# Value matmuls on half the array's columns each, in a two-layer attention and MLP kernel

## The chip, the cores and the metric

The kernel runs on one core of a Trainium2 chip. The metric is the device time of one execution in microseconds; where several runs are shown, their median. A core has a matrix engine (PE, with its weight loads shown apart as PEld), a vector engine (DVE), a scalar engine (ACT), a general engine (POOL) and a queue engine for transfers (SP). Each works through its own list of instructions in order, and they wait for one another through semaphores. Matmuls write to PSUM, which has 8 banks of 128 partitions by 512 floats.

## What is computed

Four residual blocks in a row on one sequence of 2048 rows of 512: attention, MLP, attention, MLP, with the same weights for both attentions and for both MLPs.

```python
def _A_ref(x, wqkv, wo):
    B, S, D = x.shape
    H = 32; Dh = D // H
    qkv = (x @ wqkv).reshape(B, S, 3, H, Dh).transpose(2, 0, 3, 1, 4)
    q, k, v = qkv[0], qkv[1], qkv[2]
    scores = jnp.einsum("bhqd,bhkd->bhqk", q, k) * Dh ** -0.5
    p = _softmax(scores, axis=-1)
    o = jnp.einsum("bhqk,bhkd->bhqd", p, v)
    return o.transpose(0, 2, 1, 3).reshape(B, S, D) @ wo

def _B_ref(x, w1, w2):
    return jnp.einsum("bsf,fd->bsd", _silu(jnp.einsum("bsd,df->bsf", x, w1)), w2)

x = x + _A_ref(_layernorm(x), wqkv, wo)
x = x + _B_ref(_layernorm(x), w1, w2)
x = x + _A_ref(_layernorm(x), wqkv, wo)
x = x + _B_ref(_layernorm(x), w1, w2)
```

S is 2048, D 512, the MLP's width 1792; there are 32 heads of 16. All inputs are bf16.

## The kernel before

Everything stays on the chip: the activations `x_sb`, the weights, and per layer the keys `KT` and the values `vs`. Each of the two layers runs one loop over units (line 725). A unit is a block of 512 queries (c, four of them), a group of four heads (hb, eight of them) and a block of 128 keys (kt, sixteen of them), so there are 512 units per layer and 1024 in all.

A unit has three parts. The scores (`emit_s`, line 612) are four matmuls, one per head, each over 17 rows of the array that start at row 0, 32, 64 or 96; their outputs, 128 keys by 512 queries, go in pairs into two PSUM tiles `s_ps` of two banks each, from a pool of three. The exponentials (line 732) are two ACT instructions, one per pair of heads (`pr` 0 and 1), each over 128 by 1024, from `s_ps` to the bf16 tile `p_sb`, of which there are four. The value matmuls (`emit_pv`, line 624) multiply `p_sb` by the values and add up over all sixteen key blocks in one PSUM bank `o_ps`, of which there is one. Each head owns 32 of the 128 partitions of `o_ps`: 16 for its output, one for the sum of its probabilities. To get four heads into one bank, the values are laid out in `vd`: for each head j a block of 128 columns that is zero but for the 16 columns of that head and a column of ones at 32j + 16. So every value matmul uses all 128 columns, and three quarters of them multiply zeros. `vd` holds four key blocks, in two slots; POOL refills a slot with four copies (`vd_fill`, line 142) every four units, once its last reader is done.

The order of the work on PE, ACT and DVE is the order in which the program emits it (`manual_schedule`, line 633). In the loop a unit emits its two exponentials, then the scores of the next unit, then value matmuls, then at most one piece of background work. The value matmuls of a unit's second pair are held over: at kt 1 to 15 the block has the held pair of the unit before and the first pair of this one, four matmuls in all. At kt 0 only the held pair of the last head group is emitted, after which DVE copies `o_ps` out (`finish_heads`, line 722) and the bank is reused; at kt 1 the block has six matmuls, both pairs of kt 0 and the first of kt 1. `p_sb` and `s_ps` turn over in this order: a score tile is free when the exponential that read it has ended, a probability tile when its value matmuls have.

Background work comes from two lists. `must` holds the projections that the next head group needs (`k_piece` line 255, `q_piece` lines 359 and 383, `v_piece` line 316, `heads_piece` line 397), `side` what follows for the query block before: the output projection (`epilogue_pieces`, lines 423 and 432), normalization, the MLP (`ffn_pieces`: up projection line 450, tanh on ACT line 484, down projection line 457) and the next layer's values. A rate spreads these steps over the remaining units (`pump_one`). After the loop the last query block's MLP runs by itself (`last_chunk`).

Of the kernel before, what the change touches and what calls it, by code (L numbers as in the profile page):

```python
# [12 lines left out]
BF16 = mybir.dt.bfloat16  # L13
# [5 lines left out]
def kernel(  # L19
# [10 lines left out]
    nc = tc.nc  # L30
# [5 lines left out]
    P = 128  # L36
    H = 32
    DH = D // H
    assert D == 512 and DH == 16 and S % 512 == 0 and F % P == 0
    CT = D // P  # L40
    TT = S // P
# [6 lines left out]
    NG = 4  # L48
    NR = 2
# [3 lines left out]
    xpool = ctx.enter_context(tc.tile_pool(name="xpool", bufs=1))  # L53
# [61 lines left out]
    for pad, i in ((wk_pad, 1), (wq_pad, 0)):  # L115
        for ct in range(CT):
            nc.gpsimd.tensor_copy(
                out=pad[:, ct, :, 0:DH],
# [10 lines left out]
    vs = [vpool.tile([P, TT, D], BF16, name=f"v{i}", tag="v") for i in range(2)]  # L129
    vdq = []  # L130
    for i in range(NR):
        vd = xpool.tile([P, NG, 4, P], BF16, name=f"vd{i}")
        nc.gpsimd.memset(vd[:], 0.0)
        for j in range(4):
            nc.gpsimd.memset(vd[:, :, j, 32 * j + DH : 32 * j + DH + 1], 1.0)
        vdq.append(vd)


    def vd_fill(va, hb, g, slot):
        for j in range(4):  # L140
            h = 4 * hb + j
            nc.gpsimd.tensor_copy(  # L142
                out=vdq[slot][:, :, j, 32 * j : 32 * j + DH],
                in_=va[:, NG * g : NG * (g + 1), DH * h : DH * (h + 1)],
            )

# [159 lines left out]
    def amax_bm(hb):  # L306
        nc.vector.tensor_reduce(
            out=amax[:, hb : hb + 1], in_=KT[:, hb, :], axis=AX.X, op=ALU.max,
            apply_absolute_value=True,
        )  # L310
        nc.vector.tensor_scalar_mul(out=Bm[:, hb, :], in0=E[:, :], scalar1=amax[:, hb : hb + 1])
# [192 lines left out]
    def next_pieces(c, xnTs, va):  # L504
        cell = {}
        pieces = ln_steps(c, cell)
        for tq in range(4):
            pieces.append(v_piece(lambda: cell["xnT"], 4 * c + tq, va))

        def keep():  # L510
            xnTs[c] = cell["xnT"]

        pieces.append([keep])
        return pieces
# [91 lines left out]
    def add(q, pieces):  # L606
        q += [list(p) for p in pieces]

    def emit_s(QT, hb, kt):
        tiles = [wide("s_ps") for _ in range(2)]  # L610
        for j in range(4):
            nc.tensor.matmul(  # L612
                tiles[j // 2][:, j % 2, :],
                lhsT=KT[32 * j : 32 * j + VS, hb, kt * P : (kt + 1) * P],
                rhs=QT[32 * j : 32 * j + VS, :],
                start=True,
                stop=True,
            )
        return tiles

    def emit_pv(o_ps, p_sb, kt, pr):
        for jj in range(2):
            j = 2 * pr + jj
            nc.tensor.matmul(  # L624
                o_ps[:, :],
                lhsT=vdq[kt // NG % NR][:, kt % NG, j, :],
                rhs=p_sb[:, jj, :],
                start=(kt == 0 and j == 0),
                stop=(kt == TT - 1 and j == 3),
            )  # L630

    ordered = {mybir.EngineType.PE, mybir.EngineType.Activation, mybir.EngineType.DVE}
# [44 lines left out]
    def v_first_out(c, on_act):  # L677
        dst = vs[0][:, 4 * c : 4 * c + 4, 0 : D // 2]
        if on_act:
            nc.scalar.copy(dst, v_pss[c][:, :, :])  # L680
        else:
            nc.vector.tensor_copy(out=dst, in_=v_pss[c][:, :, :])
# [21 lines left out]
    for L in range(2):  # L704
        va = vs[L]
        last = L == 1
        nxt = [None] * NQC
        QTn = [[None] * HB for _ in range(NQC)]
        units = [(c, hb, kt) for c in range(NQC) for hb in range(HB) for kt in range(TT)]
        attn = None  # L710
        o_ps = None
        pend = []
        acc = 0.0
        s_now = emit_s(QTs[0][0], 0, 0)
        if L == 0:
            v_first_out(NQC - 1, False)
        for i in range(NR):
            vd_fill(va, 0, i, i)

        def finish_heads(o_ps, hb, attn):  # L720
            oT = opool.tile([P, 512], BF16, name="oT", tag="oT")
            nc.vector.tensor_copy(out=oT[:], in_=o_ps[:])  # L722
            return heads_piece(oT, hb, attn)

        for u, (c, hb, kt) in enumerate(units):
            if kt == 0 and hb == 0:
                new_attn = apool.tile([P, 4, D], BF16, name="attn", tag="attn")

            ps = []
            for pr in range(2):  # L730
                p_sb = ppool.tile([P, 2, 512], BF16, name="p_sb", tag="p")
                nc.scalar.activation(  # L732
                    p_sb[:].rearrange("p a b -> p (a b)"),
                    s_now[pr][:].rearrange("p a b -> p (a b)"),
                    ACT.Exp,
                    scale=float(SCALE),
                )
                ps.append(p_sb)

            if u + 1 < len(units):  # L740
                nc_, nhb, nkt = units[u + 1]
                s_now = emit_s(QTs[nc_][nhb], nhb, nkt)

            if kt == 0:
                for args in pend:
                    emit_pv(*args)
                heads = None
                if o_ps is not None:
                    heads = finish_heads(o_ps, (hb - 1) % HB, attn)
                if hb == 0:  # L750
                    if c > 0:
                        add(side, epilogue_pieces(c - 1, attn))
                        add(side, ffn_pieces(c - 1, emit_out=last))
                        if not last:
                            add(side, next_pieces(c - 1, nxt, vs[1]))
                    attn = new_attn
                o_ps = oppool.tile([P, 512], FP32, name="o_ps", tag="o")
                pend = [(o_ps, ps[0], 0, 0), (o_ps, ps[1], 0, 1)]
                if c == 0 and hb + 1 < HB:
                    add(must, [k_piece(xnTs, k, hb + 1) for k in range(NQC)])  # L760
                    add(must, [[lambda hb=hb: amax_bm(hb + 1)]])
                if hb + 1 < HB:
                    add(must, [q_piece(xnTs, c, hb + 1, QTs)])
                elif c + 1 < NQC:
                    add(must, [q_piece(xnTs, c + 1, 0, QTs)])
                if L == 0 and c == 0 and hb < HB // 2:
                    for tt in range(4 * hb, 4 * hb + 4):
                        add(must, [v_piece(lambda tt=tt: xnTs[tt // 4], tt, va, D // 2, D)])
                if c == NQC - 1 and hb == 1 and not last:
                    add(side, [k_first_piece(nxt, k) for k in range(NQC - 1)])  # L770
            else:
                pend.append((o_ps, ps[0], kt, 0))
                for args in pend:
                    emit_pv(*args)
                pend = [(o_ps, ps[1], kt, 1)]

            if kt % NG == 0 and u > 0 and u + NG * (NR - 1) < len(units):
                _, fhb, fkt = units[u + NG * (NR - 1)]
                vd_fill(va, fhb, fkt // NG, fkt // NG % NR)

            if kt == 1:
                if heads is not None:
                    must.insert(0, list(heads))
                continue
            left = TT - kt - (2 if kt == 0 else 0)
            remaining = left + (TT - 2) * (HB - 1 - hb)
            rate = (steps(must) + steps(side) + len(cur) + 2 * (HB - 1 - hb)) / remaining
            rate = max(rate, (steps(must) + len(cur)) / max(left - 1, 1))
            acc = min(acc + rate, 1.99)
            if acc >= 1.0:  # L790
                pump_one()
                acc -= 1.0
            if kt == TT - 2:
                while must:
                    pump_one()
        for args in pend:
            emit_pv(*args)
        run([finish_heads(o_ps, HB - 1, attn)])
        assert not must
        while side or cur:  # L800
            pump_one()
        mvs = last_chunk(NQC - 1, attn, emit_out=last)
        if not last:
            c = NQC - 1
            nxt[c] = xtpool.tile([P, CT, 512], BF16, name="xnT", tag="xt")
            for half in range(2):
                apply_transpose(mvs[half], 4 * c, [2 * half, 2 * half + 1], nxt[c], half == 0)
            xnTs, QTs = nxt, QTn
            q_first = q_piece(xnTs, 0, 0, QTs, first=True)
            k_ps = k_first_mm(xnTs[c])  # L810
            q_first[0]()
            k_first_out(k_ps, c)
            amax_first()
            for tt in (4 * c, 4 * c + 2):
                v_two(xnTs[c], tt, vs[1])
            q_first[1]()
# [28 lines left out]
```

## Time and profile before

| | |
|---|---|
| median of 3 runs | 2133.42 us (2133.16 to 2134.91) |
| the profiled execution | 2134.4 us |
| its span, first to last instruction | 2132.6 us |
| mean granted clock of PE | 0.983 |
| first exponential of layer 1, of layer 2 | 60.6 us, 1103.9 us |
| PE busy, ACT busy | 92%, 93% |

In the profile a group of instructions is one line: source line, engine, operation, output and inputs by the program's names, shapes, count; then the busy time and the mean of one in ns; then how long the engine stood idle just before such instructions, and what ended most of it. Busy times are the union of records. Matmuls are pipelined and a record shows about 379 ns of one, while the next can start 216 ns after it, so PE's busy share isn't its load. The slices divide the span in 40 equal parts and give tenths. PEclk is the share of full speed that the clock throttle granted to PE. Some value matmuls have no record (3919 of 4096).

These are the groups of the background work, which the change doesn't touch:

```profile
L457 PE MATMUL y_ps<-w_sb,hT 128*128 128x512 bf16 x440 | 115.8, 379 | 0.4
L450 PE MATMUL h_ps<-xnT,w_sb 128*128 128x512 bf16 x333 | 85.9, 379 | 0.2
L255 PE MATMUL k_ps<-xnT,wk_pad 128*128 128x512 bf16 x251 | 69.5, 398 | 3.2 <-DVE xnT L664 1.6
L359 PE MATMUL q_ps<-xnT,wq_pad 128*128 128x512 bf16 x253 | 66.4, 383 | 0.2
L484 ACT ACTIVATE t_sb<-h_ps 128x512 f32<-128x512 f32 x84 | 59.2, 705 | 0.0
```

### The profile page before, as it was taken

To read this page: it belongs to the slowest core of one execution; us is meant where nothing else is said; L and a number is where in the kernel's file an instruction comes from. 1 tells how busy PE (TensorE), PEld (TensorE's weight loads), DVE (VectorE), ACT (ScalarE), POOL (GpSimd) and SP (SyncE) were. 2 spreads that over 40 slices of the span, in tenths; PEclk is the share of its full clock that TensorE was granted. 3 is DMA by queue.
4 is the path that set the end of the run, shared out by engine and by line. 5 is a ranking of instruction groups with operands and counts; after the bars stand their busy time and mean duration, and the time that the engine had idled before them with its cause. 6 is when DMAs were issued, how large, how long until landed. Compare 5 with 4: busy or idle time off the path is not lost.

```text
span 2132.6 us, 28924 instructions
## 1 busy us (share of the span) xinstructions
PE 1964.2 (92%) x10533; PEld 722.5 (34%) x10737; DVE 549.2 (26%) x1132; ACT 1990.4 (93%) x2207; POOL 244.9 (11%) x1054
## 2 busy tenths in 40 slices
PE   4999999999999999999789999999999999999996
PEld 2333333333333333333343333333333333333334
DVE  4333223112322133212342322221113111131104
ACT  3899999999999999999649999999999999999992
POOL 2011111111111111111001111111111111111110
PEclk8999999999999999999889999999999999999998
DMA  4000000000000000000000000000000000000000
GB/s 148 1 1 1 1 1 1 1 1 1 1 1 1 1 1 1 1 1 1 1 1 1 1 1 1 1 1 1 4 8 1 1 1 8 3 1 1 3 6 13
DMA packets 9023, 11.82 MB, mean 6 GB/s; under 512 B 432, under 2 KB 8368, under 8 KB 8880
## 3 DMA queue, kind: packets, MB, share of 16 engines
q1 hardware_dynamic: 7296, 8.39, 1.2%
q8 instruction: 84, 1.38, 0.3%
q10 hardware_dynamic: 1584, 1.57, 0.2%
q14 instruction: 59, 0.48, 0.1%
HBM read 7.86 MB, written 2.10 MB: 5 GB/s over the span
## 4 chain that ended last, share of the span: by engine, by line
PE 52%; ACT 25%; issue 20%; DVE 2%; DMA 0%; ACTq 0%; SPq 0%; POOL 0%; another core or an unknown queue 0%; POOLq 0%
PE o_ps L624 25%; ACT p_sb L732 24%; PE s_ps L612 13%; PE y_ps L457 4%; PE q_ps L359 2%; PE k_ps L255 2%; PE h_ps L450 2%; PE h_ps L563 1%; ACT xn L198 1%; PE at_ps L397 1%; PE y_ps L432 1%; DVE st L150 1%; PE v_ps L316 1%; PE q_ps L383 0%; DMA x_sb<-in_A_x_dram 0%
## 5 line engine op out<-in xcount | busy, mean ns | idle before, releaser
L732 ACT ACTIVATE p_sb<-s_ps 128x1024 bf16<-128x1024 f32 x2048 | 1915.1, 1096 | 26.1 <-PE s_ps L612 13.7
L624 PE MATMUL o_ps<-p_sb,vd 128*128 128x512 bf16 x3919 | 1038.3, 383 | 18.7 <-issue 15.1
L612 PE MATMUL s_ps<-QT,KT 17*128 17x512 bf16 x4096 | 620.5, 383 | 83.7 <-ACT p_sb L732 72.9
L624 PEld LDWEIGHTS <-vd 128*128 128x128 bf16 x4096 | 317.8, 98 | 478.4 <-issue 237.2
L142 POOL COPY vd<-v 128x64 bf16<-128x64 bf16 x1024 | 231.9, 238 | 1823.1 <-PE o_ps L624 1777.7
L612 PEld LDWEIGHTS <-KT 17*128 17x128 bf16 x4096 | 164.1, 91 | 628.5 <-issue 605.9
L485 DVE SCALAR_TENSOR_TENSOR hT<-t_sb,h_ps 128x512 bf16<-128x512 f32 x84 | 57.7, 686 | 329.0 <-ACT t_sb L484 329.0
L457 PE MATMUL y_ps<-w_sb,hT 128*128 128x512 bf16 x440 | 115.8, 379 | 0.4
L722 DVE CAST oT<-o_ps 128x512 bf16<-128x512 f32 x64 | 44.3, 691 | 175.6 <-PE o_ps L624 175.6
L450 PE MATMUL h_ps<-xnT,w_sb 128*128 128x512 bf16 x333 | 85.9, 379 | 0.2
L463 DVE SCALAR_TENSOR_TENSOR x_sb<-y_ps,x_sb 128x512 bf16<-128x512 f32 x32 | 22.1, 690 | 234.2 <-PE y_ps L457 234.2
L388 DVE CAST QT<-q_ps 128x512 bf16<-128x512 f32 x64 | 44.3, 692 | 143.6 <-PE q_ps L383 143.6
L269 DVE TENSOR_SCALAR KT<-k_ps,onescol 128x512 bf16<-128x512 f32 x56 | 42.0, 751 | 137.2 <-PE k_ps L255 136.8
L255 PE MATMUL k_ps<-xnT,wk_pad 128*128 128x512 bf16 x251 | 69.5, 398 | 3.2 <-DVE xnT L664 1.6
L374 DVE CAST qc<-q_ps 128x512 bf16<-128x512 f32 x64 | 44.3, 692 | 91.3 <-PE q_ps L359 91.3
L359 PE MATMUL q_ps<-xnT,wq_pad 128*128 128x512 bf16 x253 | 66.4, 383 | 0.2
L457 PEld LDWEIGHTS <-hT 128*128 128x128 bf16 x448 | 43.8, 98 | 52.4
L403 DVE RECIPROCAL rec<-at_ps 128x16 f32<-128x16 bf16 x64 | 16.5, 258 | 166.0 <-PE at_ps L397 166.0
L484 ACT ACTIVATE t_sb<-h_ps 128x512 f32<-128x512 f32 x84 | 59.2, 705 | 0.0
L207 PE MATMUL t_ps<-ident,xn 128*128 128x128 bf16 x72 | 10.1, 293 | 47.5 <-ACT xn L198 47.0
L450 PEld LDWEIGHTS <-w_sb 128*128 128x128 bf16 x336 | 32.9, 98 | 39.6
L150 DVE BATCH_NORM_STATS2 st<-x_sb 128x6 f32<-128x512 bf16 x64 | 43.1, 673 | 3.1 <-DMA x_sb<-in_A_x_dram 2.6
(88 smaller groups left out, 658.4 us busy)
## 6 DMA issues: line engine op xcount, KB each, us to landing
w_sb<-in_B_w_dram SPq DMA_DIRECT2D x2, 1792.0 KB, 14.7
out_dram<-x_sb SPq DMA_DIRECT2D x16, 128.0 KB, 1.7
x_sb<-in_A_x_dram SPq DMA_DIRECT2D x3, 512.0 KB, 9.5
wraw<-in_A_wqkv_dram ACTq DMA_DIRECT2D x2, 512.0 KB, 5.8
x_sb<-in_A_x_dram SPq DMA_DIRECT2D x2, 256.0 KB, 4.1
wv_sb<-in_A_wqkv_dram ACTq DMA_DIRECT2D x1, 512.0 KB, 9.5
wo_sb<-in_A_wo_dram SPq DMA_DIRECT2D x1, 512.0 KB, 9.5
```

The source lines that it names most:

```text
L142: nc.gpsimd.tensor_copy(out=vdq[slot][:, :, j, 32 * j : 32 * j + DH], in_=va[:, NG * g : NG * (g + 1), DH * h : DH * (h + 1)],)
L150: nc.vector.bn_stats(st[:], x_sb[:, tt, :])
L255: nc.tensor.matmul(ps, lhsT=wk_pad[:, ct, 4 * hb : 4 * hb + 4, :].rearrange("p h s -> p (h s)"), rhs=xnT[:, ct, :], start=(ct == 0), stop= ...
L359: nc.tensor.matmul(cell["ps"][:, :], lhsT=wq_pad[:, ct, 4 * hb : 4 * hb + 4, :].rearrange("p h s -> p (h s)"), rhs=xnTs[c][:, ct, :], star ...
L374: nc.vector.tensor_copy(out=qc[:], in_=cell["ps"][:, :])
L450: nc.tensor.matmul(ps, lhsT=w1_sb[:, ct, ft * P : (ft + 1) * P], rhs=xfT[:, ct, :], start=(ct == 0), stop=(ct == CT - 1),)
L457: nc.tensor.matmul(ps, lhsT=hT[:, ft, tq * P : (tq + 1) * P], rhs=w2_sb[:, ft, :], start=(ft == 0), stop=(ft == FT - 1),)
L484: nc.scalar.activation(t_sb[:], hc["ps"][:, :], ACT.Tanh, scale=0.5)
L485: nc.vector.scalar_tensor_tensor(out=cell["hT"][:, ft, :], in0=t_sb[:], scalar=1.0, in1=hc["ps"][:, :], op0=ALU.add, op1=ALU.mult,)
L612: nc.tensor.matmul(tiles[j // 2][:, j % 2, :], lhsT=KT[32 * j : 32 * j + VS, hb, kt * P : (kt + 1) * P], rhs=QT[32 * j : 32 * j + VS, :], ...
L624: nc.tensor.matmul(o_ps[:, :], lhsT=vdq[kt // NG % NR][:, kt % NG, j, :], rhs=p_sb[:, jj, :], start=(kt == 0 and j == 0), stop=(kt == TT - ...
L732: nc.scalar.activation(p_sb[:].rearrange("p a b -> p (a b)"), s_now[pr][:].rearrange("p a b -> p (a b)"), ACT.Exp, scale=float(SCALE),)
```

## The change

The blocks of `vd` get 64 columns per head instead of 128. Heads 0 and 1 (the first pair) write partitions 0 to 63 of `o_ps`, heads 2 and 3 partitions 64 to 127; within its half, a head still owns 32 partitions, so the layout of `o_ps` stays as it was. `emit_pv` now takes the whole list of pending pairs. It sorts their matmuls by half and emits them in turns, a matmul of the second pair first, then one of the first pair, until both lists are empty. The first matmul of each half opens its accumulation and the last one closes it. The number of matmuls, weight loads and POOL copies stays; the block at kt 0 has matmuls of one half only, the block at kt 1 two of one half and four of the other.

```diff
-        vd = xpool.tile([P, NG, 4, P], BF16, name=f"vd{i}")
+        vd = xpool.tile([P, NG, 4, 64], BF16, name=f"vd{i}")
         nc.gpsimd.memset(vd[:], 0.0)
         for j in range(4):
-            nc.gpsimd.memset(vd[:, :, j, 32 * j + DH : 32 * j + DH + 1], 1.0)
+            nc.gpsimd.memset(vd[:, :, j, 32 * (j % 2) + DH : 32 * (j % 2) + DH + 1], 1.0)
...
-                out=vdq[slot][:, :, j, 32 * j : 32 * j + DH],
+                out=vdq[slot][:, :, j, 32 * (j % 2) : 32 * (j % 2) + DH],
...
-    def emit_pv(o_ps, p_sb, kt, pr):
-        for jj in range(2):
-            j = 2 * pr + jj
+    def emit_pv(pend):
+        halves = [[], []]
+        for o_ps, p_sb, kt, pr in pend:
+            for jj in range(2):
+                halves[pr].append((o_ps, p_sb, kt, pr, jj))
+        order = []
+        while halves[0] or halves[1]:
+            for h in (1, 0):
+                if halves[h]:
+                    order.append(halves[h].pop(0))
+        for o_ps, p_sb, kt, pr, jj in order:
             nc.tensor.matmul(
-                o_ps[:, :],
-                lhsT=vdq[kt // NG % NR][:, kt % NG, j, :],
+                o_ps[64 * pr : 64 * pr + 64, :],
+                lhsT=vdq[kt // NG % NR][:, kt % NG, 2 * pr + jj, :],
                 rhs=p_sb[:, jj, :],
-                start=(kt == 0 and j == 0),
-                stop=(kt == TT - 1 and j == 3),
+                start=(kt == 0 and jj == 0),
+                stop=(kt == TT - 1 and jj == 1),
             )
...
-                for args in pend:
-                    emit_pv(*args)
+                emit_pv(pend)
```

More of the change, by code (lines that the diff above doesn't have):

```diff
@@ L772 @@
                 pend.append((o_ps, ps[0], kt, 0))
-                for args in pend:
-                    emit_pv(*args)
+                emit_pv(pend)
                 pend = [(o_ps, ps[1], kt, 1)]
@@ L795 @@
                     pump_one()
-        for args in pend:
-            emit_pv(*args)
+        emit_pv(pend)
         run([finish_heads(o_ps, HB - 1, attn)])
```

## The prediction

> **What bounds the kernel now.** I read the page's busy table first, then its slices, then the group table.
>
> ```profile
> PE 1964.2 (92%) x10533; PEld 722.5 (34%) x10737; DVE 549.2 (26%) x1132; ACT 1990.4 (93%) x2207; POOL 244.9 (11%) x1054
> ...
> PE   4999999999999999999789999999999999999996
> ...
> ACT  3899999999999999999649999999999999999992
> ...
> PEclk8999999999999999999889999999999999999998
> ...
> L732 ACT ACTIVATE p_sb<-s_ps 128x1024 bf16<-128x1024 f32 x2048 | 1915.1, 1096 | 26.1 <-PE s_ps L612 13.7
> L624 PE MATMUL o_ps<-p_sb,vd 128*128 128x512 bf16 x3919 | 1038.3, 383 | 18.7 <-issue 15.1
> L612 PE MATMUL s_ps<-QT,KT 17*128 17x512 bf16 x4096 | 620.5, 383 | 83.7 <-ACT p_sb L732 72.9
> L624 PEld LDWEIGHTS <-vd 128*128 128x128 bf16 x4096 | 317.8, 98 | 478.4 <-issue 237.2
> ```
>
> Two engines look full. Outside the start, the layer change near the middle and the tail, ACT and PE are both at nine tenths. The exponentials (L732) decide: 2048 of them, with only 26.1 us of idle in front of them in all. By the ends of their records, undisturbed ones follow each other every 0.915 us and a tanh (L484, x84) adds 0.49: 2048 x 0.915 + 84 x 0.49 = 1915 us. The two attention stretches last 979 us (first exp 60.6 to last end 1040.0) and 978 us (1103.9 to 2081.7). So about 40 us in them is ACT being late, and no quicker PE can win more than that. PE looks full because it always has a little too much; the timeline tells what one unit (four heads, one block of 128 keys) costs it.
>
> ```profile
> 1001.49 0.71 PE L612 MATMUL s_ps<-QT,KT 17*128 17x512 bf16 x4
> ...
> 1002.13 1.04 PE L624 MATMUL o_ps<-p_sb,vd 128*128 128x512 bf16 x4
> ...
> 1003.10 0.39 PE L612 MATMUL s_ps<-QT,KT 17*128 17x512 bf16 x2
> 1003.64 0.39 PE L612 MATMUL s_ps<-QT,KT 17*128 17x512 bf16 x2 [0.15 <-ACT p_sb L732]
> ```
>
> A unit lasts two exponentials, 1.83 us. The second pair of score matmuls can start only when an exp has freed its PSUM tile (the wait on ACT). From there it is 0.32 us to the first value matmul, 0.216 between value matmuls, and 0.31 from the last one back to scores (1003.10 - 1002.13 = 0.97 for the block). PE needs 0.32 + 0.97 = 1.29 us of each 1.83; background work (four matmuls of 0.216 in a heavy step) fills the rest.
>
> The third view is the clock, in stretches of 3.41 us, because that is how long the granted clock stays put.
>
> ```profile
> 119.40:122.81 3.41, 3.41 (x25) 1.61 (x23) 0.85 (x2) 3.41 (x5) 0.00 (x0) 1.00 0.02 5
> 122.81:126.22 3.41, 2.53 (x13) 0.76 (x13) 0.69 (x1) 3.41 (x4) 0.91 (x4) 1.00 0.00 0
> 126.22:129.64 3.42, 3.42 (x12) 0.98 (x11) 0.00 (x0) 2.90 (x4) 0.00 (x0) 0.50 0.00 0
> 129.64:133.05 3.41, 3.41 (x25) 1.36 (x23) 1.16 (x3) 3.18 (x5) 0.45 (x2) 1.00 0.00 0
> 153.53:156.94 3.41, 2.69 (x15) 0.77 (x13) 0.98 (x2) 3.41 (x5) 0.90 (x4) 1.00 0.00 0
> ...
> 1136.56:1139.98 3.42, 2.69 (x13) 0.85 (x14) 0.69 (x1) 3.32 (x4) 0.90 (x4) 1.00 0.00 0
> 1139.98:1143.40 3.42, 3.42 (x12) 0.99 (x11) 0.00 (x0) 3.21 (x4) 0.00 (x0) 0.50 0.02 5
> 1143.40:1146.80 3.40, 3.40 (x25) 1.34 (x23) 1.37 (x3) 2.96 (x4) 0.45 (x2) 1.00 0.00 0
> ```
>
> The columns are length, then PE, weight loads, DVE, ACT and POOL busy with their instructions, then the granted clock. Nothing here stands idle for 3 us, yet after a stretch with 13 matmuls (122.81, 1136.56) the next runs at 0.50; after one with 15 (153.53) it stays at 1.00. Counting a matmul as 0.213 us of streaming, matmuls that run together once: 122.81 has four score pairs and four value matmuls (one without a record), 1.70 us or 0.50 of the stretch; 153.53 comes to 0.53. At full clock, streaming less than about half of such a stretch costs the clock of the next. In the half-clock stretch and the one after it ACT lost 0.52 + 0.23 = 0.75 us, and 0.21 + 0.44 = 0.65 us.
>
> **The change, part by part.** *Value matmuls at 64 columns, halves alternating.* Their number stays 4096, and so do their rows and the 512 moving columns. No row shows 64 columns. The bounds on a pair: both halves start together, as the four score matmuls do on four row groups (3 to 4 ns between starts), or one after the other, 0.216 apart as now. I take together, because the score row is the nearest case of parts of the array used side by side. The block shrinks from 0.97 to 0.216 + 0.31 = 0.53 us, and a unit from 1.29 to 0.85. At kt 0 only one half has work (two matmuls, serial as now); at kt 1 six matmuls take four slots. Weight loads: 98 ns each in the shadow of a 216 ns matmul; bounds 0 and 0.098 exposed per load, I take 0.
>
> The Trainium skill, "TensorE: Matmul & The Clock Gate", Part 3, says a weight load overlaps running matmuls only where the row group differs, which speaks against this change; the L624 rows, all on the same 128 rows, load while the previous matmul runs, so the trace does not bear it out. By the rule two loads per block would be exposed, some 0.2 us, and the unit would save 0.24 instead of 0.44.
>
> *A new array switch.* Full-width work behind a value block now follows another shape. The known switch costs 0.31 - 0.216 = 0.10 us; some 450 places, 45 us of PE against 0.43 x 960 = 413 saved. It lies in PE's new slack: nothing.
>
> *Fills and clearing.* The 1024 POOL copies (238 ns) keep their size and only change place; DMAs, SP, ACT and DVE keep their instructions. The two clearings of vd (1.81 us each at 10.6) halve, but POOL then waits 13.2 us for the first value copy anyway: nothing.
>
> *The wait at kt 2.* By the ends, 18.9 of the 40 us lie before the first exp of kt 2, 64 times 0.30. It overwrites the probabilities of kt 0, which the deferred value matmuls read: freed PSUM tile, 0.05 + 0.32 to the block, 0.23 to its second matmul, 0.38 until that ends, 0.1 to ACT, 1.08 against 0.915 for the exp between. The matmul meant is now fourth in line but in the second slot: no gain (serial: 0.43 x 64 = 28 us lost).
>
> *Gain.* What remains is 40 - 19 = 21 us, of which some 6 lie in the half-clock openings of the two layers. I take 15; bounds 0 and 21.
>
> *The clock, which is late next.* A unit without background work streams two score pairs and two value slots, 4 x 0.213 = 0.85 of 1.83, or 0.47 (before: 1.28, 0.70). That is under the point where the trace loses its clock. I halved the value streaming in each of the 569 stretches of 3.41 us inside attention, by the matmul records: the median falls from 0.80 to 0.59, and 17% come under 0.50, some 25% under 0.53. A slowed stretch is itself busy enough to win the clock back, so 78 to 110 stretches are slowed; I take 90. Price of one: at half clock a bare unit is about 1.5 us, under 1.83, so 0; with a heavy step the scores come 0.05 + 0.53 + 0.96 + 4 x 0.43 + 0.1 + 0.6 = 4.0 us after an exp freed the tile and are due three exps after it, at 2.75, so 1.25. The measured pair, with four serial value matmuls and little else, is 0.65 to 0.75. I take 0.45, below it, because the block is shorter now: 90 x 0.45 = 40 us; bounds 78 x 0.1 = 8 and 110 x 0.75 = 83.
>
> The skill's Part 1 of the same page has the clock fall after an idle stretch of about 3.4 us and advises against gaps over 3 us. The two rows above fall without one, so I go by the rows. By the rule no stretch here qualifies and the sum would be 2134 - 15 = 2119.
>
> *Sum.* The profiled execution took 2134.4 us (span 2132.6 and 1.8 around it), 1.0 above the median. 2134.4 - 15 + 40 = 2159; at the median, 2158.
>
> **The rivals.** *A: faster, the clock holds.* If what the clock watches is not streaming time (the number of matmuls is unchanged), or the level is below 0.45, the 40 us drop out: 2133 - 15 = 2118. For it: 57.96 to 61.37 had about 0.46 by my count and kept its clock. Against: the two rows above. It decides from fewer than 30 slowed stretches (30 x 0.45 = 14, the gain).
>
> *B: the halves don't run side by side.* Four slots stay, kt 2 loses 28 us, and the new switches (45 us of PE, a third reaching ACT) 15: 2133 + 43 = 2176. PE stays busy and the clock holds. For it: no row shows columns split. Against: the row groups overlap.
>
> *C: gain and clock loss cancel,* 33 slowed stretches: 2133.
>
> **How the numbers follow.** Forecast 0.50, A 0.29, B 0.11, C 0.10. The forecast's own range is 2133 - 15 + 8 = 2126 to 2133 + 83 - 15 = 2201. The whole range takes in A with its gain at 21 (2112) and ends at 2200. About 0.2% (4 us) is what a measurement tells from no change. Faster 0.30 (A, a little of the forecast's low end), same 0.12, slower 0.58.
>
> **What would show it.** The PEclk row of the slices falling to 7 or 8 in attention, and 3.41 us stretches alternating 1.00 and 0.50, prove the clock step; a steady 9 proves A. Value matmuls starting in pairs a few ns apart, and blocks of 0.53 us, prove the pairing; 0.216 throughout proves B. The wait before the first exp of kt 2 should stay near 0.3 us. I am wrong if PE is seen waiting on ACT at full clock throughout.

## The result, and the profile after

The changed kernel takes 2247.98 us (median of 4 runs, 2238.95 to 2251.1) against 2133.89: slower, ratio 1.0526 with a 95% interval of 1.0512 to 1.0541. The profiled execution has a span of 2249.3 us and a mean granted clock of 0.832, where it was 0.983.

From the page of the changed kernel, three rows of the slices and the groups of the attention loop (the exponentials are now at L741, the value matmuls at L633):

```profile
PE   4898899889988999889789889898899898998897
...
ACT  3899998999999999999459998989999999998993
...
PEclk8888867898878988998877886868987879877888
...
L741 ACT ACTIVATE p_sb<-s_ps 128x1024 bf16<-128x1024 f32 x2048 | 1921.6, 1101 | 114.1 <-PE s_ps L612 66.5
L612 PE MATMUL s_ps<-QT,KT 17*128 17x512 bf16 x4096 | 711.4, 437 | 217.3 <-ACT p_sb L741 207.6
L633 PE MATMUL o_ps<-p_sb,vd 128*64 128x512 bf16 x4096 | 797.1, 457 | 0.8 <-ACT p_sb L741 0.8
```

The clock row, nearly all 9 inside attention before, now shows 6 to 8 in most slices. ACT's idle time before the exponentials went from 26.1 to 114.1 us: 66.5 of it waits for scores, 44.0 for a value matmul whose probabilities the exponential overwrites. At the same time PE's waits for ACT before the scores went from 72.9 to 207.6 us. The two now wait for each other in turn. A record of a score matmul lasts 437 ns on average and one of a value matmul 457, where both were 383 before.

At a full clock the change does what it says. This is the timeline of PE in the changed kernel, over one unit without background work:

```profile
601.51 0.39 PE L612 MATMUL s_ps<-QT,KT 17*128 17x512 bf16 x2 [0.53 <-ACT p_sb L741]
601.84 0.62 PE L633 MATMUL o_ps<-p_sb,vd 128*64 128x512 bf16 x4
602.43 0.39 PE L612 MATMUL s_ps<-QT,KT 17*128 17x512 bf16 x2
```

The block of four value matmuls begins 0.33 us after the second score pair and is back at scores after 0.59 us, where it took 0.97. By the records the four start at 601.836, 601.839, 602.076 and 602.079: two pairs, 3 ns apart within a pair. PE now needs 0.92 us of a 1.83 us unit and waits 0.53 us for ACT in each.

What follows is the clock in stretches of 3.41 us. The columns are as in the prediction (length; PE, weight loads, DVE, ACT, POOL busy with their instructions; granted clock), and the last two are DMA:

```profile
601.27:604.68 3.41, 2.62 (x16) 0.75 (x16) 2.31 (x7) 3.41 (x5) 0.46 (x2) 1.00 0.00 0
604.68:608.09 3.41, 2.91 (x12) 0.77 (x12) 1.17 (x5) 3.22 (x4) 0.48 (x3) 0.50 0.00 0
608.09:611.51 3.42, 3.42 (x17) 0.84 (x14) 1.81 (x10) 2.80 (x4) 0.00 (x0) 0.50 0.02 5
611.51:614.92 3.41, 3.41 (x16) 0.88 (x14) 0.68 (x2) 3.02 (x4) 0.47 (x2) 0.50 0.00 0
614.92:618.33 3.41, 3.11 (x24) 0.98 (x24) 2.35 (x6) 2.74 (x4) 0.53 (x2) 1.00 0.00 0
```

A thin stretch (601.27, PE recorded busy for 2.62 us, much of it single score pairs) is followed by not one but three at half clock, although PE is recorded busy all through the second and third. ACT loses 0.19, 0.62, 0.39 and then, at full clock again, 0.67 us. PE's timeline inside these stretches shows what a unit with four small transposes in it costs at half clock:

```profile
609.41 0.98 PE L612 MATMUL s_ps<-QT,KT 17*128 17x512 bf16 x4
610.33 1.06 PE L633 MATMUL o_ps<-p_sb,vd 128*64 128x512 bf16 x4
611.32 0.61 PE L397 MATMUL at_ps<-ident,oT 128*128 128x128 bf16 x4
611.86 0.61 PE L612 MATMUL s_ps<-QT,KT 17*128 17x512 bf16 x4
```

From one set of scores to the next it is 2.45 us, against 1.83 that ACT needs for the unit.

### The profile page after: what moved, and what is told of

Read it like the earlier page. It is cut to its first block, busy times and chain, and to the rows that moved or that the text cites. A ratio compares the mean times of both kernels' runs of the same rounds, so it can differ in the third digit from the quotient of the medians.

```text
span 2249.3 us, 29064 instructions
## 1 busy us (share of the span) xinstructions
PE 1963.7 (87%) x10737; PEld 567.6 (25%) x10737; DVE 549.2 (24%) x1132; ACT 2005.2 (89%) x2207; POOL 249.3 (11%) x1054
## 4 chain that ended last, share of the span: by engine, by line
PE 61%; ACT 27%; issue 9%; DVE 3%; DMA 0%; ACTq 0%; SPq 0%
ACT p_sb L741 25%; PE o_ps L633 22%; PE s_ps L612 18%; PE y_ps L457 4%; PE q_ps L359 4%; PE h_ps L450 3%; PE k_ps L255 3%; PE v_ps L316 1%; PE h_ps L563 1%; PE y_ps L432 1%; PE at_ps L397 1%; ACT t_sb L484 1%; ACT xn L198 1%; PE q_ps L383 1%; DVE st L150 1%
## 5 line engine op out<-in xcount | busy, mean ns | idle before, releaser
L741 ACT ACTIVATE p_sb<-s_ps 128x1024 bf16<-128x1024 f32 x2048 | 1921.6, 1101 | 114.1 <-PE s_ps L612 66.5
L612 PE MATMUL s_ps<-QT,KT 17*128 17x512 bf16 x4096 | 711.4, 437 | 217.3 <-ACT p_sb L741 207.6
L633 PE MATMUL o_ps<-p_sb,vd 128*64 128x512 bf16 x4096 | 797.1, 457 | 0.8 <-ACT p_sb L741 0.8
L612 PEld LDWEIGHTS <-KT 17*128 17x128 bf16 x4096 | 177.4, 93 | 869.2 <-issue 839.3
L633 PEld LDWEIGHTS <-vd 128*64 128x64 bf16 x4096 | 174.1, 117 | 312.4 <-issue 293.7
L457 PE MATMUL y_ps<-w_sb,hT 128*128 128x512 bf16 x448 | 126.1, 403 | 0.0
L450 PE MATMUL h_ps<-xnT,w_sb 128*128 128x512 bf16 x336 | 113.0, 471 | 0.0
L359 PE MATMUL q_ps<-xnT,wq_pad 128*128 128x512 bf16 x256 | 88.3, 481 | 0.0
L255 PE MATMUL k_ps<-xnT,wk_pad 128*128 128x512 bf16 x256 | 83.9, 461 | 2.7 <-DVE xnT L673 1.6
L457 PEld LDWEIGHTS <-hT 128*128 128x128 bf16 x448 | 34.9, 100 | 81.0 <-issue 58.4
```

The source lines that it names most:

```text
L255: nc.tensor.matmul(ps, lhsT=wk_pad[:, ct, 4 * hb : 4 * hb + 4, :].rearrange("p h s -> p (h s)"), rhs=xnT[:, ct, :], start=(ct == 0), stop= ...
L359: nc.tensor.matmul(cell["ps"][:, :], lhsT=wq_pad[:, ct, 4 * hb : 4 * hb + 4, :].rearrange("p h s -> p (h s)"), rhs=xnTs[c][:, ct, :], star ...
L450: nc.tensor.matmul(ps, lhsT=w1_sb[:, ct, ft * P : (ft + 1) * P], rhs=xfT[:, ct, :], start=(ct == 0), stop=(ct == CT - 1),)
L457: nc.tensor.matmul(ps, lhsT=hT[:, ft, tq * P : (tq + 1) * P], rhs=w2_sb[:, ft, :], start=(ft == 0), stop=(ft == FT - 1),)
L612: nc.tensor.matmul(tiles[j // 2][:, j % 2, :], lhsT=KT[32 * j : 32 * j + VS, hb, kt * P : (kt + 1) * P], rhs=QT[32 * j : 32 * j + VS, :], ...
L633: nc.tensor.matmul(o_ps[64 * pr : 64 * pr + 64, :], lhsT=vdq[kt // NG % NR][:, kt % NG, 2 * pr + jj, :], rhs=p_sb[:, jj, :], start=(kt == ...
```

## The experiments

"Lateness" below is worked out from the records of each run: the time from the end of one exponential or tanh in attention to the end of the next, less the undisturbed 0.916 us for an exponential and 0.49 for a tanh. It was 40 us in the kernel before and is 158 us in the changed one. The difference of 118 agrees with the 117 us between the two profiled executions (2251.1 and 2134.4); the medians differ by 114. "Slowed" counts the 3.41 us stretches of attention at half clock. The ratio is to the kernel before on the same chip, with its 95% interval.

| kernel | time, us (ratio, 95%) | clock | slowed | lateness, us | of it before the first exp of kt 2 |
|---|---|---|---|---|---|
| before | 2134 | 0.983 | 5 | 40 | 19 |
| changed | 2248 (1.0512 to 1.0541) | 0.832 | 205 | 158 | 51 |
| half of the value matmuls, 128 columns | 2217 (1.0324 to 1.0456) | 0.819 | 217 | 115 | 23 |
| alternating order, 128 columns | 2148 (1.0041 to 1.0086) | 0.982 | 6 | 53 | 34 |
| 64 columns, order of before | 2248 (1.0474 to 1.0595) | 0.842 | 191 | 148 | 54 |
| changed, a filler pair in each block | 2161 (1.0061 to 1.0157) | 0.960 | 36 | 68 | 33 |
| changed, two filler pairs in thin units and at kt 0 | 2136 (0.9994 to 1.0013) | 0.980 | 9 | 43 | 35 |
| the same, without kt 0 | 2129 (0.9953 to 0.9977) | 0.975 | 13 | 34 | 19 |
| changed, five probability tiles, no filler | 2217 (1.0362 to 1.0403) | 0.838 | 195 | 124 | 16 |
| five tiles, filler in thin units and at kt 0 | 2110 (0.9866 to 0.9896) | 0.980 | 9 | 16 | 6 |
| five tiles, filler in thin units | 2105 (0.9849 to 0.9879) | 0.981 | 8 | 9 | 0 |
| five tiles, one filler pair in thin units | 2122 (0.9925 to 0.9954) | 0.961 | 33 | 27 | 2 |
| before, five tiles | 2116 (0.9901 to 0.993) | 0.981 | 6 | 23 | 0 |

**Thin PE without column halves.** This is the kernel before with two of four value matmuls per block left out, so that the values of half of the heads are missing from its output (the other changed lines give the missing heads a sum to divide by and close the accumulation):

```diff
-        for jj in range(2):
+        for jj in range(1):
             j = 2 * pr + jj
...
```

> The kernel before at 128 columns, with the second head of each pair left out of the value matmuls (two of four per block; the values of 16 of 32 heads are not computed). PE streams as little per unit as in the changed kernel, without any column halves. Theory 1 (thin PE streaming costs the clock, and the clock costs the time): mean granted clock 0.80 to 0.86, 2220 to 2260 us. Theory 2 (the 64-column form itself is what costs): clock 0.97 or more, 2105 to 2134 us.

Measured 2217 us at clock 0.819. From its page:

```profile
PEclk8889767888878987898887886778987769866788
...
L734 ACT ACTIVATE p_sb<-s_ps 128x1024 bf16<-128x1024 f32 x2048 | 1906.7, 1092 | 80.6 <-PE s_ps L614 61.3
...
L626 PE MATMUL o_ps<-p_sb,vd 128*128 128x512 bf16 x2048 | 756.0, 457 | 5.8 <-POOL vd L144 4.3
```

The matmuls are 128 columns wide, there are half as many, and the picture is that of the changed kernel: the same 457 ns mean, a clock row much like it, a similar wait for scores (61.3 us against 66.5). Less work on PE made the kernel 3.9% slower. The form of the matmul is not needed to explain the loss. The time lies just under the expected band; at kt 2, where this kernel has fewer matmuls to wait for, ACT was late by 23 us instead of 51.

**The order alone.** This is the alternating order at 128 columns. Against the changed kernel, the layout of `vd` goes back to that of before, and one accumulation covers all columns again:

```diff
...
-                o_ps[64 * pr : 64 * pr + 64, :],
+                o_ps[:, :],
...
```

> The kernel before at 128 columns with the alternating order alone. Theory 1: clock stays near 0.98; the matmul that the first exp of kt 2 waits for is fourth in a serial line instead of second, 64 x 0.43 = 28 us, so 2155 to 2170 us. Theory 2 (order doesn't matter): 2130 to 2138 us.

Measured 2148 us: 14.0 us over the 2134.1 us of the kernel before on the same chip, half of what was expected. The waits of ACT in this kernel (from, to: us in total, times, longest):

```profile
ACT p_sb L741 <- PE o_ps L633: 28.4, 67, 1.2
```

Before, this wait was 9.5 us. By the records the first exp of kt 2 starts 0.92 us after the first value matmul of its block, and 0.70 before: one slot of 0.216 later, and 64 x 0.216 = 13.8 us. So the exp waits for the third matmul in the line and not the fourth: it starts 0.10 us after the end of the third, as it started 0.10 after the end of the second before. The third is the last reader of the other pair of kt 0, so the exp seems to be given that pair's tile in this order, where the prediction had taken the tile for fixed. Which tile it writes no record shows.

**64 columns in the old order.**

```diff
-        while halves[0] or halves[1]:
-            for h in (1, 0):
-                if halves[h]:
-                    order.append(halves[h].pop(0))
+        order = [(*args, jj) for args in pend for jj in range(2)]
```

> 64 columns with the order of the kernel before: two matmuls of one half, then two of the other, so only the middle two can run together and a block streams three slots instead of two. Theory 1: about 0.58 of a unit without background work is streaming, just over the level; clock 0.95 or more, 2115 to 2150 us. Theory 2 (the form costs): 2230 us or more.

Measured 2248 us at clock 0.842, as slow as the changed kernel: the number that theory 2 named. But the kernel with half of the value matmuls had lost most of that without its reason, the 64-column form. The timeline of PE in this kernel:

```profile
599.61 0.62 PE L625 MATMUL o_ps<-p_sb,vd 128*64 128x512 bf16 x4
...
601.44 0.63 PE L625 MATMUL o_ps<-p_sb,vd 128*64 128x512 bf16 x4
```

A block of four takes 0.62 us here too, from first start to last end. Its starts by the records are 601.444, 601.451, 601.684 and 601.691. If each half's second matmul had held up the other half, the block would have taken three slots, 2 x 0.216 + 0.38 = 0.81 us. So, by the timing, PE paired the matmuls by itself: one of the second half in line started beside the first of the first half, ahead of a matmul that stands before it in the program. The records don't say which matmul is which; that a pair is made of both halves follows from the full-width blocks, where two matmuls on the same columns start 0.216 us apart. Over all blocks of four, the two of a pair start 7 ns apart here and 3 in the changed kernel. The alternation isn't what makes the pairs, and the run doesn't give the three-slot density that it was made for. With PE as thin as in the changed kernel, the slow clock is what theory 1 asks for.

**More work for PE.** A tile of zeros is multiplied into both halves in the middle of each block of four, and within each block of two; the sums don't change:

```diff
+            if n == {1: 9, 2: 1, 4: 2, 6: 9}[len(order)]:
+                for h in (1, 0) * 1:
+                    nc.tensor.matmul(
+                        o_ps[64 * h : 64 * h + 64, :], lhsT=zw[:], rhs=p_sb[:, 0, :],
+                        start=False, stop=False, skip_group_check=True,
+                    )
...
```

> The changed kernel with a pair of value matmuls by a tile of zeros put into each block of four (and of two), which adds nothing to the output: more work for PE. Theory 1: three slots per block keep the clock at 0.95 or more and the time falls to 2115 to 2150 us. Theory 2: more matmuls of the costly form, 2250 us or more.

Measured 2161 us at clock 0.960: 1920 extra matmuls took 87 us off the changed kernel. That is the direction of theory 1, though 10 us above its band: 36 stretches were still slowed, which fits three slots putting a bare unit near the level (0.58 of streaming, as the expectation has it).

**Filler where PE is thin.** Two pairs go in after the value block of a unit whose background step has fewer than two matmuls (counted by `heavy`), and after the block at kt 0:

```diff
...
             if kt == 0:
                 emit_pv(pend)
+                if o_ps is not None:
+                    emit_fill(o_ps, 2)
...
+            if kt > 1 and heavy[0] - was < 2:
+                emit_fill(o_ps, 2)
...
```

> The changed kernel with two pairs of 64-column matmuls by zeros after the value block of every unit whose background step has fewer than two matmuls; the output is the same. Theory 1 (the clock alone made it slow): granted clock 0.975 or more, fewer than 15 slowed stretches in attention, 2115 to 2136 us, since the work is not thinner than before anywhere and heavy units are 0.43 us shorter. Rival (64 columns, the switch of array shape or the new order cost something of their own): 2145 us or more at a full clock.

Measured 2136 us. From its page:

```profile
PEclk8999999999999999999889999999999999999998
...
L757 ACT ACTIVATE p_sb<-s_ps 128x1024 bf16<-128x1024 f32 x2048 | 1913.1, 1178 | 38.2 <-PE o_ps L642 27.7
```

The clock is back at 0.980 with 9 slowed stretches, and the 5% are gone; the time equals that of the kernel before. So the loss was the clock's. But no gain is left, and the last column of the table says where it went: 35 us of the 43 lie before the first exp of kt 2. Elsewhere the lateness fell from 21 to 8. More kernels follow this up.

> The thin-unit filler with four probability tiles, without the two pairs at kt 0. Theory 1: the filler at kt 0 made the scores of kt 2 late (0.54 us before the first exp of kt 2 instead of 0.30 before the change); without it that wait is 0.30 to 0.35 again, 64 x 0.2 = 13 us less than with it, 2118 to 2126 us, and so faster than the kernel before at the same clock (0.97 or more): the columns bring some 13 us at a full clock. Rival (the columns bring nothing even at a full clock): 2131 to 2140 us.

Without the filler at kt 0, which stood ahead of the scores of kt 2, the wait there is back at 19 us. The time is 2129 us, less by 7 us than with it and a little over the expected band. The clock accounts for that: the profiled execution has 13 slowed stretches instead of 9, and of its ten runs the three at a clock of 0.980 or 0.981 took 2121 to 2124 us, inside the band, the seven at 0.970 to 0.975 2129 to 2133.

> The changed kernel with five probability tiles and no filler. Theory 1: the clock stays at 0.82 to 0.85 because PE is as thin as in the changed kernel; of the 51 us that ACT was late before the first exp of kt 2 at least half goes, 2195 to 2225 us. Rival (kt 2 only shows what PE lost elsewhere): 2240 us or more.

Five probability tiles without filler: 2217 us, clock 0.838. The lateness at kt 2 falls from 51 to 16 us, and the clock stays as it was.

> As the run before, with five probability tiles p_sb instead of four, so that the first exp of kt 2 no longer waits for the deferred value matmuls. Theory 1: the 19 us that stand before this exp go as well, 2095 to 2118 us. Rival (the lateness at kt 2 comes from PE and only moves to the scores): within 5 us of the run before.

> As the run before with five probability tiles. Theory 1: 2100 to 2110 us, some 3 to 6 us under the version with filler at kt 0. Rival (kt 0 is thin enough to lose the clock without filler): clock under 0.97 and 2112 us or more.

With both, 2110 us, and 2105 us without the filler at kt 0; both as theory 1 had it. From the page of the latter, the fastest kernel here:

```profile
PEclk8999999999999999999889999999999999999999
...
L757 ACT ACTIVATE p_sb<-s_ps 128x1024 bf16<-128x1024 f32 x2048 | 1913.6, 1300 | 11.5 <-PE s_ps L621 11.1
...
L652 PE MATMUL o_ps<-wv_sb,zw 128*64 128x512 bf16 x2188 | 333.1, 384 | 0.0
```

The last line is the filler, 2188 matmuls by zeros. ACT's idle time before the exponentials is 11.5 us, two thirds of it in the first 35 us of attention in the two layers.

> As e10 with one pair of filler per thin unit instead of two. Theory 1: three slots per unit leave 0.58 streaming, just over the level, so some stretches are slowed: clock 0.95 to 0.975, 2108 to 2130 us, slower than e10. Rival (less filler leaves PE more room and the clock holds): 2095 to 2105 us.

One pair instead of two: 2122 us, clock 0.961, 33 slowed stretches. Less work on PE, and 17 us more.

**How much of this is the columns'.** This is the kernel before with a fifth tile; room is made for it in two other buffers:

```diff
-    ppool = ctx.enter_context(tc.tile_pool(name="ppool", bufs=4))
+    ppool = ctx.enter_context(tc.tile_pool(name="ppool", bufs=5))
...
-    xnpool = ctx.enter_context(tc.tile_pool(name="xnpool", bufs=3))
+    xnpool = ctx.enter_context(tc.tile_pool(name="xnpool", bufs=2))
...
-            qu = qwork.tile([P, 512], BF16, name="qu", tag="qu")
+            qu = qc
```

> The kernel before, 128 columns and its own order, with five probability tiles; room is made by taking the absolute value of the queries in place and by two tiles xn instead of three. Theory 1: the 19 us before the first exp of kt 2 go, the other 21 stay: 2113 to 2120 us at clock 0.98. Rival (PE is too full at 128 columns to use the fifth tile): 2128 us or more.

Measured 2116 us. From its page:

```profile
L732 ACT ACTIVATE p_sb<-s_ps 128x1024 bf16<-128x1024 f32 x2048 | 1910.7, 1142 | 15.3 <-PE s_ps L612 15.1
```

Of the 30 us that the best version wins, 19 come from the fifth tile and would have been had at 128 columns; 2116.0 - 2105.0 = 11 us come from the 64 columns, and only with the filler.

## Why the prediction was right in kind and wrong in size

*What bounds the kernel, and the pairing.* Right. ACT's exponentials bound it, and the halves run side by side. Block and unit shrank to 0.59 and 0.92 us, with 0.53 and 0.85 forecast; the return to the scores takes 0.36 instead of 0.31 from the last start. The weight loads stay in the shadow of the matmuls, as taken: they have a median of 109 ns at 64 columns, against 98 at 128, and the second pair of a block starts 0.24 us after the first.

*The gain of 15.* Right in size, at a full clock: the lateness outside kt 2 is 8 us with the filler (before 21), and the columns' share of the best version is 11 us.

*The clock falls when PE streams less than about half of a stretch.* Right. Counted as in the prediction over the changed kernel's records (0.213 us from each recorded start, twice that at half clock, what runs together once), all 45 stretches at full clock under 0.50 were followed by half clock, and none of 228 at 0.60 or more; between 0.50 and 0.60, 41 of 128. The runs of slowed stretches number 88, with 78 to 110 forecast for stretches that lose the clock. That this number came out is partly luck: of the 86 full-clock stretches in this count that lost it, 41 lie above 0.50, and the prediction doesn't show how its 17% and 25% of 569 become 78 and 110.

*"A slowed stretch is itself busy enough to win the clock back."* This is the step that failed. Before, all four that streamed 0.9 or more of their time did. In the changed kernel 117 of 205 were followed by another slowed one, and a run lasted 2.3 on average. Their streaming share has a median of 0.86, and of the 171 between 0.80 and 0.90, 78 won the clock back and 93 did not. I had two examples of recovery, both with blocks of four, and carried them over to blocks of two. The kernel with half of the value matmuls, counted in the same way, puts the level for this near 0.90: 65 of 70 slowed stretches at 0.90 or more won the clock back, and 29 of 147 below. With 205 instead of 90 the same price makes 205 x 0.45 = 92 us, and the forecast would have been 2133 - 15 + 92 = 2210.

*The price of 0.45 per slowed stretch.* Too low: (118 + 13) / 205 = 0.64, where 13 is the gain that the loss had to eat up as well. That is just under what the two stretches of before had shown, 0.65 to 0.75. (The price is worked out from the loss, so that both terms together make the 131 proves nothing.) I had gone below it because the block is shorter at half clock; it is, but two other things weigh more. A straight-line fit to the lateness of the 88 runs of slowed stretches, each with the stretch after it, gives about 0.04 us per slowed stretch, 0.26 for each background matmul of 512 columns in it, and 0.96 for each first exp of kt 2. The bare unit costs next to nothing, as forecast. The forecast had charged nothing for kt 2.

*"No gain, no loss at kt 2".* Right only at a full clock. For 32 of the 64 the clock was full in the 3 us before, and the wait had a median of 0.29 us; the other 32, with half clock in that time, make up 41 of the 51 us, where the sum was 19 before. It is part of the 118.

*Rival A* is excluded by the clock row, *rival B* by the starts of the pairs, and *rival C*, with its 33 slowed stretches, by the 205. B's price at kt 2 was mis-sized as well: 14 us measured, 28 said.

The Trainium skill has the clock fall in "TensorE: Matmul & The Clock Gate" (Part 1) after an idle stretch, as the prediction quoted; the advice on gaps stands in the table of its section "Why this matters for your kernels". Another section of the page, "A second HAM failure mode: psum-queue depth-cycling", tells of a kernel whose short idle times between groups of matmuls make the clock go to and fro. This case looks like that one, though here PE waits for ACT: no wait in the thin unit above is over 0.53 us, and in the 86 stretches that lost the clock PE was never idle for more than 1.02 us at a time. Part 3 of the same page has matmuls start in program order without exception; the run in the old order shows 0.62 us where that rule needs 0.81, so by the timing it doesn't hold between column halves here.

What stays open: what exactly the throttle counts, since my count leaves a mixed band from 0.50 to 0.60; and why the recovery at a share of 0.80 to 0.90 goes either way. That two slots per block fill a slowed stretch less than four did is the likely reason that the clock stays low, but no run varies this alone. With one filler pair in thin units, 9 of 33 slowed stretches were followed by another, against 117 of 205 without filler.

## What to carry to other kernels

Before making matmuls cheaper on an engine that waits for another one anyway, count how much of each few microseconds it will still stream; where that falls toward half, expect the saved work to return as half clock and to stay, as here. Then the saved time is worth something only if the matmul engine is kept busy (zeros will do). What the narrower tiles freed in space, a fifth buffer here, was worth having but didn't bring the clock back: 2217 us without filler. And look for the one wait that repeats: 64 times 0.30 us at kt 2 was worth more than halving the largest matmul group.

## What the runs showed of the hardware

Taking half of the value matmuls away made the kernel 3.9% slower, and adding 1920 useless ones to the changed kernel made it 87 us faster. In share of time the clock takes less to keep than to win back: in the changed kernel all 228 stretches with 0.60 or more of streaming at full clock kept it, while none of the 18 with 0.65 to 0.80 at half clock won it back. In matmuls it is not so, since a share of 0.80 at half clock is only 0.40 of what a full-clock stretch can hold. And matmuls on two column halves pass each other, by the timing: the pairs were 3 to 7 ns apart whether the program alternated the halves or not.
